# Attention and a routed expert layer in one kernel: scatters through separate views of the output, splits at a slot's beginning, routing tables in PSUM

## The chip, the cores and the metric

The kernel runs on one core of a Trainium2 chip. The metric is the device time of one execution in microseconds (us). The engines are TensorE (PE in the profile; its weight loads are PEld), VectorE (DVE), ScalarE (ACT), GpSimd (POOL) and SyncE (SP), which here only starts transfers. Each engine runs its own queue of instructions in order and waits on semaphores for the others.

## The reference, cut to what matters

```
# q, k, v, alpha: 4 batches x 8 heads x 768 steps x 48
for t in range(S):
    state = alpha[:, :, t, :, None] * state + k[:, :, t] (x) v[:, :, t]
    y[:, :, t] = q[:, :, t] . state
x = y as 3072 rows of 384
logits = x @ w_gate + modality_bias[modality_id]     # 8 experts
e = argmax(logits);  gate = softmax(logits)[e]
out[row] = gate * (relu(x[row] @ w1[e]) @ w2[e])     # w1: 384x1024, w2: 1024x384
```

## The kernel before, in words

The work has two halves.

**The attention loop** (to about 104 us of the profile) goes over 24 chunks of 128 steps, mostly two at a time ("units", `n` in the code). VectorE turns the decays of a unit into factors by two scans in the PSUM tile `GF` (`decay`, `decay_back`) and scales k and q with them; TensorE computes transposes, scores, outputs and state updates of the unit before; ScalarE moves results out of PSUM; GpSimd masks the scores (`affine_select`, L385), forms products for the scans (L315), scales queries (L322) and updates the state tile `T` (L451). In between, the rows that are finished are routed: small operations on VectorE find each row's expert (`route_flow`, L561 to L601) and the list of rows of the first expert served (`route_early`, L684 to L721), with small matmuls on TensorE (L570 to L576, L678, L714). Their tables (`mx`, `eq`, `hsum`, `hr`, `key0`, `OHE`, each a few columns) lie in SBUF. The routing of rows 0 to 1023, 1024 to 2047 and 2048 to 2559 falls into the loop, that of the rest behind it.

**The experts** (from about 130 us) are served in slots: two early ones of 256 rows (0 and 1), then slots 2 to 5 and 7 of 512 rows, and a short one of up to 32 rows (6, kind "H"). For a slot, rows are gathered by GpSimd's indirect DMA (L859) and their gates likewise (L865). Rows and weights are split into a high and a low float32r part, and every product is three matmuls (L1319 to L1321, L1300 to L1302). Layer 1 of a slot has eight groups of nine matmuls, each into one PSUM buffer of the ring `tr`, which has three; ScalarE makes hH of it (L989) and VectorE hL (L991). Layer 2 has one group per block of 128 rows; ScalarE scales it by the gate into `os` (L1334), and `put` (L1241) scatters `os` into `out` by indirect DMA from GpSimd's queue. All 24 scatters are declared to write the same tensor `out`, so each waits until the one before has landed; the last one stands in a branch (L1529 to L1552).

The rows of slots 3, 4, 5 and 7 are turned by `halves_turned`: GpSimd copies the 16-bit halves of the words apart (eight copies, L1275), four transposing DMAs of SP's queue turn them (L1279), ScalarE puts the words together again (L1290) and makes xH (L1291), VectorE makes xL (L1292). It is a generator in steps. In the loop over slots, the copies for slot n + 2 are issued when slot n has stored its second block:

```
            if u == 1:
                for i in rows:
                    if seq[i][0] == "S":
                        turning[i] = halves_turned(i % NX)
                        next(turning[i])
```

The transposes follow at the beginning of slot n + 1, ahead of the load of the weights W1 for slot n + 3; the rest is spread over the blocks of slot n + 1's layer 2. The parts of the next slot's W1 are split there too (`split1`, w1H on ScalarE L1007, w1L on VectorE L1009): parts 0 and 1 behind block 2, parts 2 and 3 behind block 3, just before the next slot's hL. The order on all five queues is the program's order, written by hand. At the end of a slot, the gates of a slot that uses the same row buffer are gathered (L1491 to L1493), which falls behind slot 4's last scatter.

## Time and profile before

| | us |
|---|---|
| median of 3 runs | 338.07 |
| the three runs | 336.88, 338.07, 341.75 |
| the profiled execution's own time | 337.49 |
| its span, first to last instruction | 335.8 |
| TensorE busy, weight loads busy | 317.1 (94%), 279.0 (83%) |
| VectorE, ScalarE, GpSimd busy | 208.6 (62%), 190.3 (57%), 185.1 (55%) |

The busy share of an engine is a mean over both halves, which have different limits. Matmuls are pipelined, so TensorE counted as busy is not TensorE at its peak. A wait is put down to the engine that, by the profile, came last.

### The profile page before, as it was taken

To read this page: it belongs to the slowest core of one execution; us is meant where nothing else is said; L and a number is where in the kernel's file an instruction comes from. 1 tells how busy PE (TensorE), PEld (TensorE's weight loads), DVE (VectorE), ACT (ScalarE), POOL (GpSimd) and SP (SyncE) were. 2 spreads that over 40 slices of the span, in tenths; PEclk is the share of its full clock that TensorE was granted. 3 is DMA by queue.
4 is the path that set the end of the run, shared out by engine and by line. 5 is a ranking of instruction groups with operands and counts; after the bars stand their busy time and mean duration, and the time that the engine had idled before them with its cause. 6 is when DMAs were issued, how large, how long until landed. Compare 5 with 4: busy or idle time off the path is not lost. (4 is left out here: it accounts for less than half of the span.)

```text
span 335.8 us, 8692 instructions
## 1 busy us (share of the span) xinstructions
PE 317.1 (94%) x3417; PEld 279.0 (83%) x3418; DVE 208.6 (62%) x379; ACT 190.3 (57%) x344; POOL 185.1 (55%) x259
## 2 busy tenths in 40 slices
PE   7898999999888999999999999989999999999991
PEld 3686888888787878999889988978899888888991
DVE  6997998999995669783671585156517651175200
ACT  3776877887756542664444843574457444664210
POOL 6879799999655350665777286674325701220121
PEclk9999999999999999999999999999999999999998
DMA  7998996889957697994048858749634833100010
GB/s 236 415 347 270 293 310 220 248 267 284 339 186 248 193 307 255 353 358 130 1 103 239 294 116 267 276 104 252 208 120 105 242 95 121 47 30 0 23 51 32
DMA packets 44038, 67.04 MB, mean 200 GB/s; under 512 B 15993, under 2 KB 30488, under 8 KB 43988
## 3 DMA queue, kind: packets, MB, share of 16 engines
q1 hardware_dynamic: 37652, 53.50, 50.7%
q0 software_dynamic: 4000, 9.68, 8.5%
q10 hardware_dynamic: 2336, 3.22, 2.6%
q8 instruction: 29, 0.48, 0.6%
q14 instruction: 21, 0.17, 0.2%
HBM read 53.79 MB, written 9.50 MB: 188 GB/s over the span
## 5 line engine op out<-in xcount | busy, mean ns | idle before, releaser
L1241 POOL DMA_INDIRECT out_dram<-os,odx x23 | 24.6, 1070 | 86.5 <-ACT os L1334 58.5
L1300 PE MATMUL sc<-w2H,hH 128*128 128x384 f32 x192 | 64.8, 338 | 0.0
L1302 PE MATMUL sc<-w2H,hL 128*128 128x384 f32 x192 | 64.3, 335 | 0.0
L1301 PE MATMUL sc<-w2L,hH 128*128 128x384 f32 x192 | 64.3, 335 | 0.0
L989 ACT ACTIVATE hH<-tr 128x512 fp32r<-128x512 f32 x47 | 28.1, 598 | 50.4 <-PE tr L1321 44.3
L1321 PE MATMUL tr<-xH,w1L 128*128 128x512 f32 (+1 forms) x144 | 53.7, 373 | 1.0 <-DVE w1L L1009 1.0
L1319 PE MATMUL tr<-xH,w1H 128*128 128x512 f32 (+1 forms) x144 | 53.9, 374 | 0.0
L1320 PE MATMUL tr<-xL,w1H 128*128 128x512 f32 (+1 forms) x144 | 53.5, 372 | 0.0
L991 DVE SCALAR_TENSOR_TENSOR hL<-tr,hH 128x512 fp32r<-128x512 f32 x47 | 32.3, 690 | 31.1 <-ACT hH L989 31.1
L1292 DVE TENSOR_TENSOR xL<-xg,xH 128x512 fp32r<-128x512 f32 x12 | 11.7, 978 | 45.5 <-ACT xH L1291 45.5
L859 POOL DMA_INDIRECT xg<-xd,idx x25 | 28.0, 1119 | 21.6 <-DVE vals L646 13.0
L1300 PEld LDWEIGHTS sc<-w2H,hH 128*128 128x128 f32 x192 | 36.0, 188 | 1.2 <-issue 1.0
L1301 PEld LDWEIGHTS sc<-w2L,hH 128*128 128x128 f32 x192 | 36.1, 188 | 0.3
L1334 ACT ACTIVATE os<-sc,gg 128x384 f32<-128x384 f32 x23 | 13.4, 582 | 40.5 <-PE sc L1302 40.3
L1302 PEld LDWEIGHTS sc<-w2H,hL 128*128 128x128 f32 x192 | 36.0, 188 | 0.1
L385 POOL TENSOR_SCALAR_AFFINE_SELECT scT<-scT 128x512 f32<-128x512 f32 x48 | 30.1, 661 | 8.3 <-ACT scT L384 8.3
L865 POOL DMA_INDIRECT gg<-gd,idx x25 | 26.7, 1068 | 10.5 <-issue 6.1
L1321 PEld LDWEIGHTS tr<-xH,w1L 128*128 128x128 f32 x144 | 27.1, 188 | 6.4 <-DVE w1L L1009 1.8
L1320 PEld LDWEIGHTS tr<-xL,w1H 128*128 128x128 f32 x144 | 27.1, 188 | 4.7
L1319 PEld LDWEIGHTS tr<-xH,w1H 128*128 128x128 f32 x144 | 27.1, 188 | 4.5
L1009 DVE TENSOR_TENSOR w2L<-w2r,w2H 128x768 fp32r<-128x768 f32 x24 | 27.4, 1142 | 0.7
L1009 DVE TENSOR_TENSOR w1L<-w1r,w1H 128x768 fp32r<-128x768 f32 x24 | 22.2, 966 | 8.3 <-ACT w1H L1007 8.2
(266 smaller groups left out, 611.7 us busy)
## 6 DMA issues: line engine op xcount, KB each, us to landing
w1r<-in_moe_w_dram SPq DMA_DIRECT2D x16, 768.0 KB, 6.7
w2r<-in_moe_w_dram SPq DMA_DIRECT2D x16, 768.0 KB, 7.3
ta<-in_turned_dram SPq DMA_DIRECT2D x11, 512.0 KB, 5.4
tk<-in_turned_dram SPq DMA_DIRECT2D x11, 512.0 KB, 4.7
tq<-in_turned_dram SPq DMA_DIRECT2D x11, 512.0 KB, 6.0
vt<-in_rowsv_dram SPq DMA_DIRECT2D x11, 384.0 KB, 4.9
xd<-xs ACTq DMA_DIRECT2D x7, 384.0 KB, 5.6
xd<-w2r SPq DMA_DIRECT2D x2, 768.0 KB
```

The source lines that it names most:

```text
L385: pool.affine_select(s, s, [[0, NP], [1, P]], ALU.is_ge, 0.0, base=0, channel_multiplier=-1)
L859: pool.indirect_dma_start(xg[x][:, u], None, xd[0:rows], IOA(idx[:, c : c + 1], 0), bounds_check=rows - 1, oob_is_err=False)
L865: pool.indirect_dma_start(gg[x][:, u : u + 1], None, gd[0:rows], IOA(idx[:, c : c + 1], 0), bounds_check=rows - 1, oob_is_err=False)
L989: act.activation(hH, hp, AF.Relu)
L991: vec.scalar_tensor_tensor(hL, hp, 0.0, hH.bitcast(F32), op0=ALU.max, op1=ALU.subtract)
L1009: vec.tensor_tensor(lw, src, hi.bitcast(F32), op=ALU.subtract)
L1300: pe.matmul(op, hH[:, us] if f is None else hH[:, f, us], wH, start=first, stop=False)
L1301: pe.matmul(op, hH[:, us] if f is None else hH[:, f, us], wL, start=False, stop=False)
L1302: pe.matmul(op, hL[:, us] if f is None else hL[:, f, us], wH, start=False, stop=final)
L1319: pe.matmul(hp, wH[:, d, fs], XH[:, d, :n], start=(d == 0), stop=False)
L1320: pe.matmul(hp, wH[:, d, fs], XL[:, d, :n], start=False, stop=False)
L1321: pe.matmul(hp, wL[:, d, fs], XH[:, d, :n], start=False, stop=(d == ND - 1))
```

## The change

Three things are changed together.

1. Each scatter is given a view of `out` of its own, taken from a list of views that are declared not to overlap. No scatter waits for the landing of another any more.
2. The copies of `halves_turned` for the next slot are issued at the beginning of a slot, the transposes behind the first weight load there, instead of the copies in the middle of the slot before and the transposes at the beginning.
3. The small routing tables of the loop lie in unused columns of the PSUM tile that holds `GF`, as long as the loop runs (`beside()` says so); a copy of `rev` is put there once, in unit 6.

```diff
-    GT = lps.tile([P, K2], F32, name="GF")[:W]
+    GTP = lps.tile([P, K2], F32, name="GF")
+    GT = GTP[:W]
+    def spare(n, dt=F32):        # the next n unused columns
+        a = free[0]
+        free[0] += n
+        return GTP[:, a : a + n].bitcast(dt)
...
+    pmx, prev_, phs = spare(8), spare(E), spare(E)
+    peq = spare(8 * E).rearrange("p (t e) -> p t e", e=E)
+    phr = spare(8, I32)
+    pkey = spare(2)
+    pOHE = spare(2 * EARLY[0]).rearrange("p (t c) -> p t c", c=2)
+    def beside():
+        return ring["rt"][0] is lps
...
-        vec.tensor_reduce(mx[:, s], L[:, s], axis=AX.X, op=ALU.max)
-        vec.tensor_tensor(ls[:, s], L[:, s], wide(mx), op=ALU.subtract)
+        tmx = pmx[:, :n] if beside() else mx[:, s]
+        vec.tensor_reduce(tmx, L[:, s], axis=AX.X, op=ALU.max)
+        vec.tensor_tensor(ls[:, s], L[:, s], tmx.unsqueeze(2).broadcast_to(sh), op=ALU.subtract)
...
-        vec.scalar_tensor_tensor(eq[:, s], ls[:, s], 0.0, over(rev), op0=ALU.is_equal, op1=ALU.mult)
-        vec.tensor_reduce(m2[:, s], eq[:, s], axis=AX.X, op=ALU.max)
-        st["chosen"] = vec.tensor_tensor(oh[:, s], eq[:, s], wide(m2), op=ALU.is_equal)
+        teq, trev = (peq[:, :n], prev_) if beside() else (eq[:, s], rev)
+        vec.scalar_tensor_tensor(teq, ls[:, s], 0.0, over(trev), op0=ALU.is_equal, op1=ALU.mult)
+        vec.tensor_reduce(m2[:, s], teq, axis=AX.X, op=ALU.max)
+        st["chosen"] = vec.tensor_tensor(oh[:, s], teq, wide(m2), op=ALU.is_equal)
...      # likewise ths for hsum, thr for hr, and:
+        tk, tO = (pkey, pOHE) if beside() and n <= EARLY[0] else (key0, OHE)
+        vec.tensor_scalar(tk, iof[:, :2], off, None, op0=ALU.add)
         vec.tensor_tensor(
-            OHE[:, :n],
-            key0.unsqueeze(1).broadcast_to([P, n, 2]),
+            tO[:, :n],
+            tk.unsqueeze(1).broadcast_to([P, n, 2]),
...
+            OHE[:, :n], tO[:, :n], tok16[:, :n].unsqueeze(2).broadcast_to([P, n, 2]), op=ALU.mult
...
+        if n == 6:
+            vec.tensor_copy(prev_, rev)
...
+    apart = iter(dram_disjoint_views(out, U * SU + 2))
-    def put(c, t):
-        return pool.indirect_dma_start(out, IOA(odx[:, c : c + 1], 0), t, None, ...)
+    def put(c, t, to=out):
+        return pool.indirect_dma_start(to, IOA(odx[:, c : c + 1], 0), t, None, ...)
...      # every store of the slots: to=next(apart)
-        if m in turning:
+        if m and m > 2:
+            turning[m] = halves_turned(m % NX)
             next(turning[m])
         coming = slot_weights(w, expert(seq[n + 2][1])) if n + 2 < len(seq) else iter(())
         next(coming, None)
+        if m in turning:
+            next(turning[m])
...
-            if u == 1:
-                for i in rows:
-                    if seq[i][0] == "S":
-                        turning[i] = halves_turned(i % NX)
-                        next(turning[i])
...
+    final = next(apart)
...
-        put(LAST, of)
+        put(LAST, of, final)
```

## Rows read from the trace of the kernel before

**Rows 1.** Windows by stage, 80 to 100 us: length, each engine's busy time (instructions), clock, DMA.
```profile
80.00:100.00 20.00, 17.77 (x410) 15.71 (x412) 18.55 (x45) 13.15 (x29) 13.95 (x21) 1.00 0.78 268
```

**Rows 2.** Waits of TensorE, 44 to 104 us: total us, times, longest.
```profile
PE y L406 <- issue: 1.0, 1, 1.0
...
PE tr L714 <- DVE OHE L708: 0.9, 1, 0.9
...
PE tr L570 <- DVE oh L567: 0.2, 1, 0.2
```

**Rows 3.** Timeline of TensorE, slot 4's beginning; in brackets the idle time before.
```profile
225.10 0.50 PE L1321 MATMUL tr<-xH,w1L 128*128 128x512 f32 x1 [1.02 <-DVE w1L L1009]
```

**Rows 4.** Lines L567, L701, L702, L708: ns min/median/max, first and last start.
```profile
L567 DVE TENSOR_TENSOR oh<-eq,m x4: 192/458/2645, 55.0 to 122.9; 128x64 bf16<-128x64 f32 x2, 128x32 bf16<-128x32 f32 x2
...
L701 DVE TENSOR_SCALAR key<-iof,off x2: 230/458/687, 96.5 to 113.7; 128x2 f16<-128x2 f32 x2
...
L702 DVE TENSOR_TENSOR OHE<-key,hi x2: 201/386/572, 97.2 to 114.0; 128x32 f16<-128x32 f16 x1, 128x40 f16<-128x40 f16 x1
...
L708 DVE TENSOR_TENSOR OHE<-OHE,tok x2: 201/377/553, 97.8 to 114.2; 128x32 f16<-128x32 f16 x1, 128x40 f16<-128x40 f16 x1
```

**Rows 5.** Line L579, its first input in SBUF (`kept`) and in PSUM (`sc`).
```profile
L579 DVE TENSOR_TENSOR rk<-kept,oh x3: 193/218/241, 63.8 to 106.8; 128x64 f32<-128x64 f32 x2, 128x32 f32<-128x32 f32 x1
...
L579 DVE TENSOR_TENSOR rk<-sc,oh x1: 184/184/184, 126.3 to 126.3; 128x32 f32<-128x32 f32 x1
```

**Rows 6.** Timeline of the end, and the wait of GpSimd's queue at L1241 there.
```profile
324.47 0.58 ACT L1334 ACTIVATE os<-sc,gg 128x384 f32<-128x384 f32 x1 [3.63 <-PE sc L1302]
...
325.33 0.97 POOL L1241 DMA_INDIRECT out_dram<-os,odx  x1 [3.24 <-ACT os L1334]
...
328.58 0.58 ACT L1334 ACTIVATE of<-sc,gg 128x384 f32<-128x384 f32 x1 [3.53 <-PE sc L1302]
330.64 0.97 POOL L1241 DMA_INDIRECT out_dram<-of,odx  x1 [4.34 <-POOLq L1529]
...
L1241 POOLq EVENT_SEMAPHORE  x1: 17/17/17, 329.9 to 329.9; - x1
```

**Rows 7.** GpSimd: timeline of one split's copies, the copies by line, a gates' gather.
```profile
170.86 4.38 POOL L1275 COPY halves<-xg 128x384 uint16<-128x384 uint16 x8
...
L1275 POOL COPY halves<-xg x8: 500/508/1222, 170.9 to 174.0; 128x384 uint16<-128x384 uint16 x8
...
262.27 1.04 POOL L865 DMA_INDIRECT gg<-gd,idx  x1 [0.30 <-issue]
```

**Rows 8.** Transposes on SP's queue in slot 3, and ScalarE's first use in slots 2, 3.
```profile
195.68 5.23 SPq L1279 DMA_TRANSPOSE turnedh<-halves  x4
...
181.38 1.41 ACT L1290 COPY xg<-turnedh 128x512 uint16<-128x512 uint16 x2 [2.62 <-DMA turnedh<-halves]
...
211.66 1.39 ACT L1290 COPY xg<-turnedh 128x512 uint16<-128x512 uint16 x2
```

**Rows 9.** VectorE: timeline of operations beside the copies, and two w1L by line.
```profile
171.17 3.72 DVE L1009 TENSOR_TENSOR w2L<-w2r,w2H 128x768 fp32r<-128x768 f32 x1
...
222.07 1.80 DVE L1292 TENSOR_TENSOR xL<-xg,xH 128x512 fp32r<-128x512 f32 x1 [3.48 <-ACT xH L1291]
...
L1009 DVE TENSOR_TENSOR w1L<-w1r,w1H x2: 946/1098/1251, 223.8 to 225.0; 128x768 fp32r<-128x768 f32 x2
```

**Rows 10.** Timeline of ScalarE and VectorE at slot 3's beginning.
```profile
190.66 0.58 ACT L1334 ACTIVATE os<-sc,gg 128x384 f32<-128x384 f32 x1 [0.17 <-PE sc L1302]
...
192.72 0.60 ACT L989 ACTIVATE hH<-tr 128x512 fp32r<-128x512 f32 x1
194.76 0.60 ACT L989 ACTIVATE hH<-tr 128x512 fp32r<-128x512 f32 x1 [1.44 <-PE tr L1321]
...
192.00 1.83 DVE L1009 TENSOR_TENSOR w1L<-w1r,w1H 128x768 fp32r<-128x768 f32 x2 [0.38 <-ACT w1H L1007]
193.75 0.68 DVE L991 SCALAR_TENSOR_TENSOR hL<-tr,hH 128x512 fp32r<-128x512 f32 x1
```

## The prediction, made before the changed kernel ran

> **What bounds the kernel now.** I first read the page's busy shares and its forty slices, then the waits of TensorE alone, because the kernel has two halves with different limits. In the first half (the attention loop, to about 104 us) VectorE looks like the limit: in the stretch from 80 to 100 us it is busy 18.55 of 20 us and TensorE 17.77 [rows 1]. But the waits of TensorE from 44 to 104 us hold almost nothing by VectorE: 0.9 us before the matmuls L714 that read OHE, and 0.2 us before L570 that reads oh [rows 2]. VectorE makes k and q about one unit ahead of their use, so its busy time is long and still not on the path, except where routing results go to TensorE. In the second half (the experts, from 130 us to the end) TensorE has one gap worth the name: 1.02 us at 225.10, before the matmul that reads w1L [rows 3]. So the time of a piece of VectorE's or GpSimd's work counts only where it reaches one of these few places, and at the end of the kernel, where the last scatter stands alone.

> **Routing scratch in PSUM.** The same small operations take very different times: the one-hot compare L567 takes 0.19 to 2.65 us, L701 0.23 or 0.69, L702 0.20 or 0.57, L708 0.20 or 0.55 [rows 4]. The long ones lie in the loop beside GpSimd's work (at 96.5, 97.2 and 97.8 for the latter three), the short ones behind it, when GpSimd has little to do. With one operand in PSUM I take the short value for each. For OHE that is 0.46 for L701, 0.37 for L702 and 0.35 for L708, together 1.18 us: more than the 0.9 that TensorE waits for it, so the whole wait goes and TensorE's own order is what is late next. The 0.2 us before L570 goes the same way, since L567 and its forerunners give back more than that. Loop: -(0.9 + 0.2) = -1.1 us; bounds 0 (the long operations stay long, or something else of the same size is waited for) and -2.1 (adding a 1.0 us gap of TensorE in front of L406 for which the profile shows no cause [rows 2]). The 2.4 us that L567 may give back in the first group is counted at nothing: no matmul waits for it there, TensorE's queue is full of attention work, which hides it. The price of a PSUM operand: the compare-and-multiply L579 takes 0.184 us with its first input in PSUM and from 0.193 us with it in SBUF, same shape [rows 5], so I take nothing, with 0.02 us each way. The added copy of rev into PSUM is one more tiny VectorE operation; I put it between 0.08 (half a short one) and 0.69 us, took 0.2, and the same cover hides it.

> [...]

> **Scatters through views declared apart.** Before, each scatter waits until the one before it has landed, since both write the same tensor. In the experts' half this delays GpSimd's queue but no matmul, so its removal earns nothing there by itself; its use is that GpSimd comes to the split's copies earlier. At the end it is on the path: the last but one scatter starts at 325.33, the queue is let go at 329.9, while the last block `of` is ready at 328.58 + 0.58 = 329.16 and the last scatter starts at 330.64 [rows 6]. Elsewhere a scatter starts 0.28 us after its block (325.33 against 324.47 + 0.58). So the gain is at most 330.64 - 329.44 = 1.2 us, and nothing if the branch's own bookkeeping, which stands between 329.9 and 330.64, sets the start. I take 0.3, as the branch is nearer and not touched.

> **Splits at a slot's beginning.** A split is eight copies on GpSimd (4.4 us together [rows 7]) and four transposing DMAs on SP's queue (5.2 us to issue [rows 8]). Before, the copies stand behind the scatter of a slot's second block, in the middle of its second layer; now they come first in the next slot, past the scatters of blocks 2 and 3. The transposes are moved behind the load of a slot's W1 on SP. Removed: in slot 3 the copies held up VectorE's xL at 222.07 (1.80 us, of which it works less than one [rows 9]) and so w1L behind it, which TensorE waited for 1.02 us [rows 3]. That gap goes: -1.0 us.

> Added: the copies now meet w1L and hL at the slot's start. What such a meeting costs is in the trace: a subtraction of two SBUF tiles issued at 171.17, 0.3 us behind the first of eight copies, took 3.72 us instead of 0.95 and ended at 174.89, 4.0 us after the copies began, while the eighth copy alone was lengthened, to 1.22 us, from 0.5 [rows 7, 9]. It is let in only ahead of the last copy. The other three splits show the same. And GpSimd does get in between two such operations of VectorE: the first w1L behind that xL took 1.25 us instead of 0.95 [rows 9].

> Now slot 3's beginning, by [rows 10]. Block 3's output is ready at 190.66 + 0.58 = 191.24; its scatter can start 0.28 us later, at 191.52, takes 0.97 [rows 6], and the copies stand ready from 192.50. VectorE then runs w1L of part 2 (192.00 to 192.95). The copies get in at 192.95, w1L of part 3 is held for 4.0 us, to 196.95, and hL (0.68 us, behind it in VectorE's queue) is ready at 197.65 instead of 194.43. The hidden layer has three PSUM buffers; its groups end 2.04 us apart (192.72 and 194.76 on ScalarE), the first at about 192.65. The fourth group starts at 192.65 + 2 x 2.04 = 196.73 and needs the buffer that hL sets free: 197.65 + 0.1 - 196.73 = 1.0 us of stall. VectorE then has 0.69 + 0.96 + 0.69 us of work until the next buffer is needed, 4 us later, so one stall per slot. Slot 4 begins by the same pattern: 2 x 1.0 = +2.0 us. Slot 2 does not: GpSimd is still busy with gathers and comes some 6 us late, when w2L meets the copies and nobody waits for that. Nor does slot 5: the four gathers of gates (1.04 + 0.3 us each [rows 7]) stand between the last scatter and its copies, so these come 5.3 us later. Bounds: 0 (w1L of part 3 slips in first) and 2 x 1.5 (both parts held: 192.50 + 4.0 + 0.95 + 0.68 + 0.1 - 196.73).

> The transposes are hidden: with copies from 193 us and W1's loads ahead of them they are issued by about 203 and land by about 208, while ScalarE first reads them in the layer's second half, at 211.66 [rows 8].

> **Sum**, against the profiled execution's own 337.49 us (span 335.8, the rest lies around it): -1.1 (loop) - 0.3 (end) - 1.0 (old gap) + 2.0 (new stalls) = -0.4, that is 337.1. The median of the runs shown is 338.07, 0.6 above the profiled run, and the three spread from 336.88 to 341.75, so I leave the sum at 337.1 and let the range reach up.

> **Rivals.** *No new stall.* The copies let VectorE in after each instruction. For it: in the loop small operations got in after one GpSimd instruction (L701, L702 and L708 each waited about one, 0.35 to 0.46 us [rows 4]). Against it: the copies of all four splits. w1L of part 3 would be held 0.5 us, within the 2.3 us that hL has to spare (196.73 - 194.43). Then the +2.0 falls away: 335.1. [...]

> *More stalls.* Both w1L parts are held in slots 3 and 4, or slots 2 and 5 are hit too, as GpSimd is no longer late: 1.2 to 2 us more, and if half of the loop's gain is not seen either, 339.3.

> *Slower.* The transposes, queued behind W1's loads, land after 211.66. VectorE's xL then pushes the next slot's first matmul. It decides from about 3 us of lateness (in slot 2 ScalarE waited 2.6 us for them and no gap of TensorE followed [rows 8]); I see 3 us of margin ahead of that (208 against 211.66), so they would have to be 6 us late. At 8 us late, 2 us in each of slots 2 to 5: 337.1 + 8 = 345.

> *The scatters still wait* (the views are taken as one): GpSimd comes late to the copies, the stalls move or go, the end gains nothing: 336 to 337.5.

> **How the numbers follow.** Forecast 0.50 (336 to 338.3); no new stall 0.28 (335.1, with the loop's larger gain 334.1); more stalls 0.13; scatters still wait 0.05; slower 0.04. The range 334.3 to 339.3 leaves out the last, the outer parts of the second and third, and some of the spread of runs. Two per cent is 6.8 us, about what a measurement of this kernel can tell from no change; only the slower rival, or three gains that I don't see, get there: faster 0.03, same 0.92, slower 0.05.

> **What will show it.** In the changed kernel: L701, L702, L708 at 0.2 us and no wait of TensorE on OHE; no 1 us gap at 225; in slots 3 and 4 a w1L of 3 to 4 us and a gap of 1 us before the fourth hidden group; the last scatter's start against `of`. It is wrong if no w1L is lengthened at the slots' starts, or if TensorE waits on xH or xL.

## The result

The changed kernel takes 332.35 us (median of 6 runs, 332.00 to 333.31), the kernel before 336.98 (6 runs beside them, 334.62 to 341.75): a ratio of 0.9888, 95% interval 0.9854 to 0.9922, so 1.1% faster and clear of noise. The forecast was 337.1 us, the range 334.3 to 339.3. The profiled execution took 332.0 us with a span of 330.2, against 335.8 before. On the chips of the experiments the executions of one kernel spread over 1 to 4%, at granted clocks of 0.97 to 1.00 (three of the kernel before, at 0.40 to 0.66, took 451 to 813 us); the ratios compare fast executions with fast ones, while the traces of g, h, i and p are of slow ones.

Windows of the changed kernel: 80 to 100 us, which answers to [rows 1], and the beginnings of slots 3 and 4, where the forecast had its new stalls.

```profile
80.00:100.00 20.00, 19.43 (x465) 17.46 (x457) 16.36 (x52) 14.28 (x33) 15.61 (x22) 1.00 0.70 235
...
187.00:196.00 9.00, 9.00 (x41) 7.39 (x40) 6.69 (x9) 5.21 (x10) 7.69 (x10) 1.00 0.75 212
220.00:229.00 9.00, 9.00 (x41) 7.39 (x40) 6.69 (x9) 5.21 (x10) 7.68 (x10) 1.00 0.80 212
```

In the loop TensorE is busy 1.66 us longer in 20 than in [rows 1], VectorE 2.19 us less. In slots 3 and 4 TensorE works 9.00 of 9.00 us: no new stall, and the gap of [rows 3] is gone too. The waits of TensorE from 44 to 104 us (all there are), then its timeline at the two places of [rows 2]:

```profile
PE tr L454 <- ACT knat L380: 0.9, 2, 0.5
PE y L416 <- POOL T L461: 0.5, 1, 0.5
PE tr L472 <- ACT kept L115: 0.3, 1, 0.3
```

```profile
86.60 0.62 PE L416 MATMUL y<-q,T 64*64 64x128 f32 x16
87.15 0.20 PE L592 MATMUL tr<-oh,tri 128*128 128x64 bf16 x1
...
95.03 0.55 PE L740 MATMUL tr<-OHE,OL 128*128 128x2 f16 x16
```

(L416, L592 and L740 are L406, L570 and L714 of before.) The waits on oh and OHE are gone, and so is the 1.0 us pause in the middle of L406. By lines, the operations of [rows 4]:

```profile
L589 DVE TENSOR_TENSOR oh<-GF,m x3: 191/224/224, 53.8 to 99.9; 128x64 bf16<-128x64 f32 x2, 128x32 bf16<-128x32 f32 x1
L589 DVE TENSOR_TENSOR oh<-eq,m x1: 192/192/192, 119.6 to 119.6; 128x32 bf16<-128x32 f32 x1
...
L728 DVE TENSOR_TENSOR GF<-GF,hi x1: 199/199/199, 93.5 to 93.5; 128x32 f32<-128x32 f32 x1
...
L734 DVE TENSOR_TENSOR OHE<-GF,tok x1: 191/191/191, 93.8 to 93.8; 128x32 f16<-128x32 f32 x1
```

All are at the short value now, among them the one that had taken 2.65 us. The timeline of the end, against [rows 6], where the last scatter began 1.48 us behind `of` (330.64 against 328.58 + 0.58); now it is 324.60 - (323.75 + 0.58) = 0.27:

```profile
320.49 0.97 POOL L1272 DMA_INDIRECT out_dram<-os,odx  x1 [3.24 <-ACT os L1365]
324.60 0.97 POOL L1272 DMA_INDIRECT out_dram<-of,odx  x1 [3.14 <-POOLq L1559]
...
323.75 0.58 ACT L1365 ACTIVATE of<-sc,gg 128x384 f32<-128x384 f32 x1 [3.53 <-PE sc L1333]
```

**Where the 5.6 us of span went.** TensorE's instructions stand in the same order in both kernels, so I compared the start of the same group in the two traces. The changed kernel is ahead by 0.46 us at 44 us, before any changed instruction (chance), by 3.38 from 95 us on (the loop gives 2.9), by 4.84 from 257 us on (the experts give 1.5, of which 1.3 at the old gap), and by 5.6 at the end (0.7 there).

### The profile page after: what moved, and what is told of

Same layout as the page of the kernel before. It is cut to its first block, busy times and chain, and to the rows that moved or that the text cites. A ratio compares the mean times of both kernels' runs of the same rounds, so it can differ in the third digit from the quotient of the medians.

```text
span 330.2 us, 8690 instructions
## 1 busy us (share of the span) xinstructions
PE 315.9 (96%) x3417; PEld 278.9 (84%) x3418; DVE 199.0 (60%) x380; ACT 190.2 (58%) x344; POOL 187.1 (57%) x259
## 4 chain that ended last, share of the span: by engine, by line
PE 61%; POOL 15%; issue 12%; DVE 6%; DMA 3%; ACT 2%; POOLq 1%; ACTq 0%; DVEq 0%
PE sc L1331 8%; PE sc L1333 8%; PE sc L1332 8%; PE tr L1352 7%; PE tr L1351 7%; PE tr L1350 7%; POOL scT L395 4%; PE tr L165 3%; PE y L428 3%; POOL pp L325 3%; POOL tq L332 2%; PE tr L390 2%; PE tr L472 2%; POOL S L459 2%; POOL out_dram L1272 2%
## 5 line engine op out<-in xcount | busy, mean ns | idle before, releaser
L1272 POOL DMA_INDIRECT out_dram<-os,odx x23 | 23.5, 1021 | 84.7 <-ACT os L1365 78.4
L1323 DVE TENSOR_TENSOR xL<-xg,xH 128x512 fp32r<-128x512 f32 x12 | 8.3, 692 | 48.5 <-ACT xH L1322 48.5
L395 POOL TENSOR_SCALAR_AFFINE_SELECT scT<-scT 128x512 f32<-128x512 f32 x48 | 28.9, 635 | 7.8 <-ACT scT L394 7.8
L1035 DVE TENSOR_TENSOR w1L<-w1r,w1H 128x768 fp32r<-128x768 f32 x24 | 23.0, 997 | 8.8 <-ACT w1H L1033 8.6
L1035 DVE TENSOR_TENSOR w2L<-w2r,w2H 128x768 fp32r<-128x768 f32 x24 | 26.4, 1100 | 0.7
```

Of the source, the lines that this page charges most:

```text
L395: pool.affine_select(s, s, [[0, NP], [1, P]], ALU.is_ge, 0.0, base=0, channel_multiplier=-1)
L1035: vec.tensor_tensor(lw, src, hi.bitcast(F32), op=ALU.subtract)
L1272: return pool.indirect_dma_start(to, IOA(odx[:, c : c + 1], 0), t, None, bounds_check=N - 1, oob_is_err=False)
```

## The experiments

The later chips show pauses of ScalarE and TensorE that the first two traces don't show; so ratios to the kernel before, each from the same chip, stand beside the readings, and what follows is read from the traces, stretch by stretch. "Lateness" is how much later than in the changed kernel's first trace (called "after") the same group of TensorE starts. The ratios can't settle the parts: their intervals reach some 0.5% (1.7 us) either way, and b and i, with most tables in SBUF, have lower ratios than the changed kernel. The loop's 2.9 us below rests on the traces alone.

### The parts alone

**a_tables**: the tables in PSUM, one shared output, splits where they were.

```diff
-    apart = iter(dram_disjoint_views(out, U * SU + 2))
+    apart = iter([out] * (U * SU + 2))
...
-        if m and m > 2:
-            turning[m] = halves_turned(m % NX)
+        if m in turning:
             next(turning[m])
```

> Only the tables in PSUM; one shared output, splits as before. The traces of the two kernels put the loop's gain at about 2.9 us (TensorE 3.38 us ahead from 95 us on, 0.46 of it before any changed instruction). Theory A (the tables earn all of it, the two pauses of TensorE that nothing explained included): 2.5 to 3 us below the kernel before, ratio 0.991 to 0.993. Theory B (the two pauses, 0.30 and 0.99 us, were chance of one execution): 1.1 to 1.6 us below, ratio 0.995 to 0.997. In both the gap of about 1 us of TensorE at the split of slot 3 stays, and the end stays as before.

Ratio 0.9952 (0.9913 to 0.9991). In the loop it runs level with the changed kernel to 97 us (lateness -0.02 at 87 us, -0.03 at 95): neither wait, no pause. So the trace is Theory A's, while the ratio lies in Theory B's range, with an interval that reaches both. In the experts' half it loses 2.5 us, 1.7 of them at slot 3's beginning, and no gap of 1 us stands at slot 4's (0.3 us).

**b_apart_splits**: `beside()` returns False, so all tables are in SBUF; the rest as changed.

> Views apart and splits at a slot's beginning, tables in SBUF as before. The two parts of the change touch different halves of the time, so if they add up: gap in slot 3 gone (1.0 us), end 0.5 to 1.2 us shorter, loop as before: 1.5 to 2.2 us below the kernel before, ratio 0.9935 to 0.9955. The forecast's own theory (a stall of 1.0 us in each of slots 3 and 4): ratio 1.000 to 1.003. If w1L gets in between the copies, its durations are about 1.2 us there and no group of the hidden layer is late.

Ratio 0.9835 (0.9788 to 0.9881). In the experts' half its lateness doesn't grow at all (5.63 from 126 to 323 us). In the loop it grows by 2.9, as the timeline of TensorE shows:

```profile
87.26 0.40 PE L416 MATMUL y<-q,T 64*64 64x128 f32 x8
88.43 0.45 PE L416 MATMUL y<-q,T 64*64 64x128 f32 x8 [0.77 <-issue]
89.27 0.20 PE L592 MATMUL tr<-oh,tri 128*128 128x64 bf16 x1 [0.39 <-DVE oh L589]
...
98.14 0.56 PE L740 MATMUL tr<-OHE,OL 128*128 128x2 f16 x16 [0.93 <-DVE OHE L734]
```

The pause in the middle of L416 is back. It was no chance of one execution. The ratio is lower than any that was expected; what the kernel before loses on that chip beyond its first trace (see before_again) would lower it.

**c_apart**: views apart alone (`beside()` False, splits where they were). **d_splits**: splits moved alone (`beside()` False, `apart` as in a_tables).

> Only the views apart; splits in the middle of a slot's second layer as before, tables in SBUF. The end gains 0.5 to 1.2 us; the gap in slot 3 may move, since GpSimd comes to the copies some microseconds earlier. If the gap needs only that the copies run back to back when VectorE asks, it stays or turns up elsewhere: ratio 0.996 to 0.999. If the gap goes as well: ratio 0.993 to 0.995.

> Only the splits at a slot's beginning; one shared output, so that each scatter still waits for the landing of the one before it and GpSimd comes late to the copies, tables in SBUF. If the views apart are needed for the splits: the copies begin 3 to 6 us into the slot, meet w2L instead of w1L, the transposes are late by the same, ratio 0.998 to 1.006 (a stall of 0 to 2 us in place of the gap of 1.0). If not: gap gone, ratio 0.996 to 0.998. The end as before.

c_apart: ratio 0.9896 (0.9854 to 0.9938). All its rows of copies in slots 2 to 4 hold xL for 3.0 us, but with the scatters out of the way they begin earlier (the second at 186.89 us, against 194.70 in the kernel before), when the next slot is not near, and no matmul waits for it; its one loss in that half is a pause at 205 us, behind 5.0 us in which ScalarE stood still for nothing that the trace names. d_splits has no ratio (4 runs, 339.76 to 346.66). It loses 2.1 us at slot 3's beginning; TensorE's waits there, and ScalarE's timeline in d and, at the same place (slot 2's third block), in a:

```profile
PE tr L1350 <- ACT w1H L1033: 1.3, 1, 1.3
PE tr L1352 <- DVE w1L L1035: 0.3, 1, 0.3
```

```profile
190.22 0.58 ACT L1365 ACTIVATE os<-sc,gg 128x384 f32<-128x384 f32 x1 [1.88 <-DMA out_dram<-os,odx]
...
188.18 0.58 ACT L1365 ACTIVATE os<-sc,gg 128x384 f32<-128x384 f32 x1 [0.49 <-remote]
```

In d ScalarE comes late to `os`, makes w1H late, and the next slot's first matmul waits. The profile puts the 1.88 us down to the landing of the scatter of the slot's first block, but the shared output is not shown as the cause. The tile `os` has four buffers, one for each block of a slot, so the third block needs none that this scatter holds; and in a, which shares the output too, the same `os` started at 188.18 us while that scatter landed only at 191.9. ScalarE also stood still for long ahead of `os` in slot 2 with views apart (at the first block 5.8 us in e and 5.7 in k, against 2.9 in after), for nothing that the traces name. Nor do c and d show which part removed the old gap: a and before_again, with shared output and the splits where they were, don't have it either, so it has been seen in one trace only. What the traces give for the experts' half as a whole is this: b loses nothing, c 1.4 us (the pause at 205), d 2.3, a 2.5. At the end, the views do show: the last scatter begins 1.35 to 1.59 us behind `of` in the four traces with a shared output (kernel before twice, a, d) and 0.27 to 0.47 in the eleven with views apart. The time from there to the end of the span doesn't shrink (4.5 to 5.1 and 4.9 to 5.9 us).

**i_list_only**: only key0 and OHE in PSUM.

```diff
-        tmx = pmx[:, :n] if beside() else mx[:, s]
+        tmx = mx[:, s]
...
-        teq, trev = (peq[:, :n], prev_) if beside() else (eq[:, s], rev)
+        teq, trev = (eq[:, s], rev)
```

> The changed kernel with only the place list's tables (key0, OHE) in PSUM; the maxima, eq, rev, the sums and the slots' tables are back in SBUF. Theory A (the loop's gain is the wait on OHE plus an earlier oh): the wait of 0.9 us on OHE is gone or under 0.3, the small operations of the route take up to 0.6 us again, and at the matmuls that read oh (87 to 90 us) TensorE is 0.5 to 1.5 us later than in the changed kernel, by a wait on oh or by a pause that covers it. Theory B (the list's tables alone do it): nothing left of the 1.46 us there. Against the kernel before 1.0 to 1.3 us of the loop's gain remains by A, 2.5 to 3 by B.

Ratio 0.9844 (0.9790 to 0.9898). In the loop, Theory A: the wait on OHE is gone, 1.46 us at the matmuls that read oh remain.

**before_again** and **k_after**: the two kernels once more.

> The kernel before once more, for a trace from the same chip as these. The wait on OHE of 0.9 us and a late oh at 87 to 90 us are there; so is a gap of about 1 us or more of TensorE at one of the splits in slots 3 to 5. A pause in the middle of L406 stands there if and only if the 16 KB of TensorE's instructions before it come when TensorE has passed some 100 instructions more than in the changed kernel's first trace.

> The changed kernel once more, beside the variants below on the same chip. 1 to 1.5 per cent under the kernel before; no pause of TensorE over 0.3 us between slots 2 and 6; w1L of parts 2 and 3 about 1.2 us each in slots 3 and 4.

before_again (one run, 345.89 us) has all that was expected of it in the loop; its largest gap in the experts' half is not at a split, but 2.7 us on `os` in slot 2, behind 6.3 us in which ScalarE stood still for nothing that the trace names; with the slower matmuls behind it (mean granted clock 0.75 from 193.8 to 197 us and 0.70 from there to 200, 1.00 ahead of them) it costs TensorE 4.6 us. k_after (4 runs, 338.70 to 344.25 us, median 342.45 against 343.57 of the kernel before on its chip, no ratio) misses the 1 to 1.5% that were expected. It has none of the two waits, and slots 2 to 6 run as expected, but it has a pause of 1.40 us in the middle of L416, in a kernel with tables in PSUM, and one of 0.81 us before that.

**e_stores_later**: as b_apart_splits, but with less traffic ahead of the pause.

```diff
-        if NN - 4 <= n < NN - 2:
-            held_out((n - NN + 4) * NF // 2, NF // 2)
+        if NN - 3 <= n < NN - 1:
+            held_out((n - NN + 3) * NF // 2, NF // 2)
```

> Tables in SBUF (as in b_apart_splits), but the two stores of the held-out rows are issued one unit of the loop later, so that 768 KB of traffic less stand ahead of TensorE's instruction fetch of 86.2 us. Theory 'fetch' (the pause of TensorE of 0.8 to 1.0 us in the middle of L416 at 87.7 us is a wait for the next 16 KB of its instructions, which a busy DMA serves some 2.5 us late): the fetch comes before 85 us and the pause is gone, TensorE is 0.8 to 1.0 us earlier from there on than in b_apart_splits. Theory 'operand' (the second half of L416 waits for something of VectorE or GpSimd): the pause stays at 0.8 to 1.0 us.

No ratio (4 runs, 341.11 to 351.45 us). Timeline of TensorE:

```profile
87.86 0.62 PE L416 MATMUL y<-q,T 64*64 64x128 f32 x16
...
89.57 0.20 PE L592 MATMUL tr<-oh,tri 128*128 128x64 bf16 x1 [1.09 <-DVE oh L589]
```

The pause is gone, the fetch came at 85.28 us, hardly later than expected, and nothing is won: TensorE now waits for oh instead. (The later stores also delay the first gather of rows, by 3.6 us of TensorE's time.)

### Rows of copies against VectorE

**g_copies_early**: the row of copies behind block 2's scatter instead of block 3's.

```diff
-        if m and m > 2:
-            turning[m] = halves_turned(m % NX)
-            next(turning[m])
...
+            if u == len(cols[n]) - 2 and mm:
+                turning[mm] = halves_turned(mm % NX)
+                next(turning[mm])
```

> The changed kernel, but the eight copies of a slot's split stand ahead of the last scatter of the slot before, right behind the scatter of block 2. GpSimd is then free when they come, so they run back to back from about 184.9 us while VectorE asks for xL at about 185.6. Theory 'already running' (VectorE waits for all but the last of copies that already run back to back when it asks, and only then): xL is held to the last copy, 3.5 to 4 us instead of 0.69, w1L of part 0 is ready 2 to 3.5 us late, TensorE stalls 2 to 3 us at the beginning of slots 3 and 4: 4 to 6 us above the changed kernel. Theory 'one copy' (VectorE gets in after each copy at these places): xL lengthened by 0.5 us at most, no stall: within 1 us of the changed kernel.

Ratio 1.0119 (1.0010 to 1.0229), the only one slower. VectorE's timeline, GpSimd's, and TensorE's waits from 185 us on:

```profile
196.76 2.98 DVE L1323 TENSOR_TENSOR xL<-xg,xH 128x512 fp32r<-128x512 f32 x1 [1.75 <-ACT xH L1322]
```

```profile
196.01 4.09 POOL L1306 COPY halves<-xg 128x384 uint16<-128x384 uint16 x8
```

```profile
PE tr L1352 <- DVE w1L L1035: 7.1, 3, 2.7
```

xL is held to the last copy (2.98 us; the piece before it took 0.69), and slots 3, 4 and 5 begin late. The mechanism of the forecast exists. TensorE loses more than it waits, 11.4 us in all: behind the waits of 2.2 us at slots 4 and 5 its matmuls stand 0.43 us apart instead of 0.23 for some 3 us. The granted clock is 0.50 from 237.5 to 240.5 us; it was 1.00 before TensorE waited, and 0.99 again from 240.5 to 245 us.

**h_copies_first**: the row ahead of block 3's scatter, started by ScalarE's writing of that block.

```diff
+        scaled = act.activation(os, op, AF.Copy, scale=gg[x][:, u : u + 1])
+        if mm:
+            turning[mm] = halves_turned(mm % NX, scaled)
+            next(turning[mm])
...
                 copy = pool.tensor_copy(hv[:, u, h], words[:, u, h])
+                if after is not None and u + h == 0:
+                    behind(copy, after)
```

> The changed kernel, but the eight copies stand ahead of block 3's scatter and wait only for ScalarE's writing of that block, so that they begin about 188.0 us, ahead of VectorE's w1L of part 2 (188.5). Theory 'already running': that w1L is held to about 192 (3.5 to 4.5 us instead of 1.2), part 3 follows, hL of the first group is about 3.5 us late, and the fourth hidden group stalls 0.7 to 1.5 us in slots 3 and 4: 1.4 to 3 us above the changed kernel. Theory 'one copy': w1L 1.2 to 1.5 us each, no stall, within 0.7 us of the changed kernel.

Ratio 0.9881 (0.9821 to 0.9942). w1L of parts 2 and 3: 1.24 and 1.25 us, and no stall at a slot's beginning. "Already running" falls: the copies did run when VectorE asked. (Elsewhere TensorE loses 1.2 us in slot 2, waiting for `os`, as in m and n, and 4.2 us in slot 3, behind 3.7 us in which ScalarE stood still for nothing that the trace names.)

**m_copies_between**: the same, the first copy waiting for w1L of part 1 as well. **n_ask_later**: m, with one more operation of ScalarE ahead of w1H of part 2.

```diff
-            turning[mm] = halves_turned(mm % NX, scaled)
+            turning[mm] = halves_turned(mm % NX, st["low"])
...
+            act.activation(os[:, :P], op[:, :P], AF.Copy, scale=gg[x][:, u : u + 1])
```

> As h_copies_first, but the first copy waits for VectorE's w1L of part 1 too, so that it begins in the 0.4 us between that subtraction and the one of part 2, with VectorE's two inputs not being read. In the ten traces so far, 23 rows of eight copies began with VectorE idle and let it in ahead of the last copy alone, and those whose first copy had to wait for a subtraction already running let it in after one or two. Theory 'first copy': w1L of part 2 now takes 3.5 to 4 us instead of 1.25, hL of the first group is some 3 us late, TensorE stalls 0.7 to 2 us before the fourth hidden group in slots 3 and 4 (slot 5 too): the stall of the forecast, 2 to 5 us above the changed kernel in all. Theory 'place' (w1L is let in because of what it reads or where it stands): 1.25 us each, no stall.

> As m_copies_between, but ScalarE scales the first third of block 3's output twice before it makes w1H of part 2, so that VectorE asks for w1L of part 2 some 0.25 to 0.3 us later: about 0.5 us after the first copy has begun, instead of 0.26. In the 52 rows of eight copies of the thirteen traces so far, each of 21 rows in which a subtraction of VectorE was running at the row's start or asked by 0.26 us let VectorE in ahead of the next copy, and each of 31 rows in which the first asked at 0.31 us or later held it to the last copy. Theory 'start of the row' (what VectorE does in the first 0.3 us settles the whole row): w1L of part 2 takes 3.3 to 3.9 us, part 3 follows with 1.25, hL of the first group is 3 us late or more, and TensorE stalls 0.7 to 1.6 us before the fourth hidden group in each of slots 3 to 5: the stall of the forecast. Theory 'place' (w1L at a slot's beginning is let in whatever its time): 1.0 to 1.3 us each and no stall.

Ratios 0.9881 (0.9831 to 0.9930) and 0.9891 (0.9846 to 0.9936). Both theories that expected a stall fall: VectorE asked 0.26 us into the row in m, 0.66 in n, and was let in ahead of the next copy both times (parts 2 and 3 together take 2.23 us in m, 2.28 in n). Timelines of n:

```profile
195.98 5.84 POOL L1306 COPY halves<-xg 128x384 uint16<-128x384 uint16 x8 [3.42 <-issue]
```

```profile
196.64 2.28 DVE L1035 TENSOR_TENSOR w1L<-w1r,w1H 128x768 fp32r<-128x768 f32 x2 [0.78 <-ACT w1H L1033]
```

What m, n and h have in common is the idle time in front of the row (3.04 us in h, 3.42 in n): GpSimd stood at a semaphore and its queue was not running. In g the copies stood queued behind a scatter in progress (195.05 to 196.02 us).

**p_early_signal**: g, with only the start of the row changed to a wait on a semaphore.

```diff
-                turning[mm] = halves_turned(mm % NX)
+                turning[mm] = halves_turned(mm % NX, st.get("half"))
...
+                st["half"] = act.copy(parts[:, h, d], tv[:, h, d])
```

> As g_copies_early (the row stands behind the scatter of block 2 and meets xL of the third piece), but the first copy waits for ScalarE's second copy of that piece's halves, which ends within 0.1 us of that scatter's end: same place, same subtraction, nearly the same moment; only GpSimd now starts the row from a wait on a semaphore. Theory 'queued row' (a row is kept to the last copy only where its copies were queued behind a running instruction of GpSimd): xL waits 0.3 us at most, as w1L did in h, m and n, and the stalls of 3 to 4 us per slot of g_copies_early are gone or under 1 us. Theory 'what asks' (xL and w2L are held, w1L is not): xL waits 2 to 2.7 us and TensorE stalls 2.5 us or more in each of slots 3 to 5, as in g_copies_early.

Ratio 0.9883 (0.9818 to 0.9948). VectorE's timeline, and TensorE's waits from 185 us on:

```profile
196.52 0.87 DVE L1325 TENSOR_TENSOR xL<-xg,xH 128x512 fp32r<-128x512 f32 x1 [3.47 <-ACT xH L1324]
197.31 4.78 DVE L1035 TENSOR_TENSOR w1L<-w1r,w1H 128x768 fp32r<-128x768 f32 x4
```

```profile
PE sc L1334 <- DVE w2L L1035: 0.6, 1, 0.6
```

Same place, same subtraction, asked 0.62 us into the row (0.75 in g): xL waits 0.18 us instead of 2.3, then VectorE and GpSimd take turns through four more subtractions, and the 7.1 us of waits are gone; slots 3 to 5 begin some 0.4 us late each. "Queued row" holds.

## Why the prediction was wrong

Against 332.0 us the forecast of 337.1 missed by 5.1, and the rival "no new stall" with the loop's larger gain, 334.1, by 2.1; by the forecast's own terms:

| term | forecast | trace |
|---|---|---|
| new stalls, slots 3 and 4 | +2.0 | 0 |
| loop | -1.1 | -2.9 |
| end | -0.3 | -0.7 |
| old gap | -1.0 | -1.3 |
| rest of the experts' half | 0 | -0.2 |
| before the first changed instruction | 0 | -0.5 |

**The step that failed is "w1L of part 3 is held for 4.0 us".** It was priced from a row in which VectorE was "let in only ahead of the last copy" [rows 7, 9], and the rival "no new stall" got 0.28. Timelines of the changed kernel at slot 3's beginning, GpSimd and VectorE, against [rows 10]:

```profile
188.04 0.98 POOL L1272 DMA_INDIRECT out_dram<-os,odx  x1 [3.18 <-ACT os L1365]
189.00 5.65 POOL L1306 COPY halves<-xg 128x384 uint16<-128x384 uint16 x8
```

```profile
188.51 2.35 DVE L1035 TENSOR_TENSOR w1L<-w1r,w1H 128x768 fp32r<-128x768 f32 x2 [0.38 <-ACT w1H L1033]
190.79 0.68 DVE L1017 SCALAR_TENSOR_TENSOR hL<-tr,hH 128x512 fp32r<-128x512 f32 x1
```

With TensorE's lead of 3.48 us taken off, scatter, row and w1L of part 2 stand where the forecast had them, to 0.1 us. But the first copy had to wait for that w1L (it took 1.05 us instead of 0.5), and from then on the two engines took turns: w1L of part 3 took 1.25 us, not 4.0. I had assumed that GpSimd, once in, keeps VectorE out. In all 60 rows of eight copies of the fifteen traces it comes to this: in 32 the first copy could begin at once, right behind a transfer that GpSimd was issuing, and VectorE's first subtraction waited 0.78 to 2.76 us, past the copies but for the last (in one row past that too); in 27 the first copy itself had to wait, in 18 for a subtraction of VectorE in progress (three of these began at a semaphore as well), in 9 at a semaphore alone, and VectorE's next one waited at most 0.31 us; one row met VectorE too late to tell. p against g shows the semaphore as a cause, with one edit. That a subtraction in progress does the same is read from 18 rows without exception and not from an edit of its own; why either of them changes the whole row stays open.

**The loop was mis-sized, and it is the term "the 0.2 us before L570".** That wait was short only because the pause of L406 stood ahead of it: lateness at the two places of [rows 2], from the point ahead of each:

| kernel | up to the matmuls on oh | up to those on OHE |
|---|---|---|
| before, before_again, b, c, d | 1.46 to 1.47 | 0.99 to 1.00 |
| e (no pause) | 1.45 | 1.00 |
| i (OHE in PSUM) | 1.46 | 0 |
| after, a, g, h, m, p | 0 | 0 |
| k, n (tables in PSUM, with the pause) | 1.62, 1.48 | 0 |

Pause and wait together cost the same 1.46 us whether 0.77, 1.2 or nothing of it is pause: take the pause away and oh is late by as much (e); have oh early and the pause alone can still cost it (k, n). In six of the eight traces with all tables in PSUM both are gone; there the faster VectorE also lets SP issue its loads earlier (in after the last store of held-out rows at 82.54 us against 86.56). That the earlier loads kept the pause off is argued: in k and n this store is as early (82.45 and 82.89 us), and the pause came all the same. To this come 0.16 us at the first matmuls on oh (57 us) and 0.25 on T at 78 us: 2.9 in all, beyond the forecast's bound of 2.1. The wait on OHE itself was right (0.9 forecast, 0.99 measured), and so was "short value for each".

**The end** was sized by "the branch is nearer": all of the bound of 1.2 us came (1.48 - 0.27), and 0.5 of it was given back behind the scatter. **The old gap** went, as forecast; that the splits' move did it is not shown, as the gap stands neither in c, where the splits are not moved, nor in a and before_again, where nothing of the experts' half is changed. **Right**: the transposes are hidden (ScalarE reads them at 208.18 us without a wait, though SP's queue held them to 197.7), slots 2 and 5 lose nothing, the PSUM operand has no visible price (the 128x32 form of L589: 0.191 us with it, 0.192 without).

## What to carry to other kernels

A wait of 0.2 us behind a pause of 1.0 us may be a wait of 1.2 us: add up what stands in a row ahead of one instruction before pricing the last of it. A price of contention read from rows that all start alike holds for that start alone (4.0 us from the rows, 1.25 in the changed kernel); ask how the moved row will start. Where VectorE must get in between GpSimd's operations, start their row from a semaphore instead of behind a running transfer (xL waited 0.18 us in p, 2.3 in g).

## What the runs showed of the hardware

**GpSimd and VectorE**: the two kinds of rows above. In the 27 rows with turns VectorE waited at most 0.31 us, against copies of 0.5; in the 32 others up to 2.76 us. An operand in PSUM has no price that L589's 128x32 form shows (0.191 us with it, 0.192 without).

| | lands at, us | pause |
|---|---|---|
| after, a, g, h, m, p | 84.2 to 84.9 | none |
| e | 86.24 | none |
| d, c, b | 86.97, 87.13, 87.19 | 1.2, 0.8, 0.8 |
| n, before, before_again, i | 87.35, 87.38, 87.49, 87.55 | 1.2, 1.0, 1.2, 1.2 |
| k | 88.08 | 1.4 |

TensorE goes on 1.2 to 1.5 us behind a late landing. The other pause of k fits as well:

```profile
83.22 0.78 PE L454 MATMUL tr<-vt,knat 128*64 128x48 f32 x22 [0.81 <-issue]
```

It stands 256 recorded instructions of TensorE ahead of the first, 1.3 us behind the landing of the twelfth packet at 81.93 us, which came by 80.92 in all other traces. The DMA engines' share is 1.06 from 86.0 to 87.5 us of the kernel before, where its thirteenth packet is late, and 0.65 from 83.05 to 84.2 us of the changed kernel, where that one fetched its own; the DMA view of the first of the two:

```profile
DMA packets 367, 0.58 MB, mean 387 GB/s; under 512 B 12, under 2 KB 358, under 8 KB 366
...
q1 hardware_dynamic: 303, 0.47, 84.7%
q10 hardware_dynamic: 63, 0.10, 16.8%
q8 instruction: 1, 0.02, 4.0%
```

Moving 768 KB of traffic out of the way (e) brought the packet forward (86.24 us against 87.19 in b) and took the pause away. That is an intervention on the traffic, not on the fetch, so the last link is argued; other pauses of the later chips (c at 205 us, ScalarE before L499 in twelve of the thirteen, all but e) have no such packet beside them and stay open.
